# Odd filter-gradient rows first, turned copies in pieces, and new row buffers and weight-load order in the tail of an adaLN spectral block

## The chip, the cores and the metric

The kernel runs on one core of one Trainium2 chip. The core has five engines with their own instruction streams: TensorE (PE in the profile, with its weight loads as PEld), VectorE (DVE), ScalarE (ACT), GpSimd (POOL) and SyncE (SP). Each runs its instructions in order; semaphores hold an instruction back until what it needs is done. DMAs are issued here from SP and from POOL. The metric is the device time of one execution in microseconds (us); lower is better. The trace is of one execution.

## The reference

The reference runs an adaLN block with two branches forward, and then its vector-Jacobian product for a given output gradient:

```python
mod = (_silu(c) @ w_mod).reshape(c.shape[0], 6, 1, -1)
sa, ca, ga, sb, cb, gb = (mod[:, 0].copy(), mod[:, 1].copy(), mod[:, 2].copy(), mod[:, 3].copy(), mod[:, 4].copy(), mod[:, 5].copy())
h = _layernorm(x, axis=-1) * (1 + ca) + sa
x = x + ga * _A_ref(h, A_w_r, A_w_i)      # irfft2(rfft2(h) * (w_r + i w_i))
h = _layernorm(x, axis=-1) * (1 + cb) + sb
x = x + gb * _B_ref(h, B_w_gate, B_w_up, B_w_down)   # ((h@gate) * (h@up)) @ down
return x
...
_out, _vjp = jax.vjp(_f, A_x, A_w_r, A_w_i, B_w_gate, B_w_up, B_w_down, c, w_mod)
return (_out0, *[jnp.asarray(_g) for _g in _grads])
```

x is 1 x 2048 x 576 in bfloat16, the spectral filter w_r, w_i is 2048 x 289, the gated branch has 4608 features, c is 1 x 576 and w_mod is 576 x 3456. The outputs are: out_0 the forward result, out_1 the gradient of x, out_2 and out_3 the gradients of w_r and w_i, out_4, out_5 and out_6 those of the gate, up and down weights, out_7 the gradient of c (576 numbers) and out_8 the gradient of w_mod (576 x 3456, an outer product of silu(c) with the six modulation gradients).

## The kernel before

Rows of x are cut into 16 tiles of 128 (NT); the 4608 features into 36 blocks of 128 ("fb", NFB). Up to about 1230 us the kernel does the forward spectral branch and a main loop over the feature blocks, which makes the weight gradients; the change does not touch it. What follows is the tail of `build`, from line 976, with three stages and an end.

**Stage 1** (`t1_norm`, `t1_out`, `t1_turn`, about 1230 to 1316 us): per tile the backward of the second normalization, a gradient tile "gx" that POOL stores to DRAM (L1223), and its transform along the columns. **Stage 2** (`t2_*`, to about 1390): per pair of frequency lanes the transform along the rows, the product with the filter, and the way back. **Stage 3** (`t3_*`, to about 1471): per tile "sa" the inverse transform, the backward of the first normalization, and the store of the out_1 tile "ob" (L1449, on POOL). **The end**: what is left of the modulation gradients.

Into these stages is dealt the final down-projection, 1152 matmuls of 128x128 by 128x288 ("u3p", L1495), 24, 24 and 21 per step, in groups of 36 that each fill one PSUM bank; ACT copies a full bank out (L1500), VectorE scales and adds (L1508, L1509) into a tile "of3", and POOL stores it to out_0 (L1514). The very first two pairs of groups (tiles 0 and 1) run side by side, matmul by matmul. The weights come in six pieces (0 to 6, 7 to 13, 14 to 20, 21 to 27, 28 to 34 and 35 of the feature blocks; `wd_load`, L1284), and the activations in loads "hl" of 9 feature blocks by 256 rows (`hl_load`, L1288), which rotate over six buffers; the first ones are issued on POOL between the gx stores, in an order written out at L1309, and later ones on SP.

**The filter gradient** (`filter_grad`, L1324) is made in 16 units: a load "Xn" of the saved spectrum, four VectorE instructions (L1330 twice, L1331, L1332), and a result in one lane of the array "wn". Even unit 2i goes to lane i (0 to 7), odd unit 2i+1 to lane 16-i (9 to 15), unit 1 to lane 8. Before, stage 2 makes the even units (from `t2_more`), its last one once more in `t2_back`, and stage 3 the odd ones, at odd sa. Two columns of each lane are halved by POOL (`scale_ends`, L1417); lanes 0 to 8 are then stored as they are (L1443, on POOL), lanes 9 to 15 must be stored in reversed row order. For that they are first written to a DRAM scratch "gback_d" (L1523, on SP) and copied from DRAM to DRAM with the rows turned (`turned_rows`, L1539, on SP), 896 rows of 578 bytes for each of out_2 and out_3.

**The modulation gradients.** For out_8, `product_rows` (L1147) lets ACT scale a gradient row by silu(c), five row blocks for each of six sections, into one five-row tile "o8" per section; two stores on SP follow the fifth row. Four sections are made in stage 2, two rows a step (L1362), the last two (MCA, MSA) at the end. For out_7, w_mod is loaded back in sections ("wmE" of 4 sections wide in three buffers, five loads; "wmL" of 2 wide in four buffers, five loads) and VectorE multiplies and sums them (`section_sum`, L1161) into a scratch tile "pr"; small steps then make the row "gcr" (L1546 to L1564).

**Order.** For TensorE, ACT and VectorE the order in the tail is written out: `deal` (L1055) strings the collected instructions together and `in_order` ties each to the one before. SP's end is tied in the same way (`end_sp`). Elsewhere the scheduler orders POOL and SP. A buffer of a pool of n is written again only when the last reader of its content n tiles back is done, a store included: `of = o2p.tile([128, D], BF, name="of3", bufs=3)` at L1506 and the `o8` tile (one buffer) at L1150 are such places.

## Time and profile before

| what | value |
|---|---|
| time, three runs | 1525.87, 1529.7, 1531.91 us; median 1529.7 |
| profiled execution | 1528.03 us, span 1526.3 us |
| mean granted TensorE clock | 0.985 |
| TensorE busy in the span | 1460.6 us (96%) |
| VectorE busy | 1047.6 us (69%) |
| ScalarE busy | 559.5 us (37%) |
| POOL busy | 233.1 us (15%) |
| HBM read, written | 105.14 MB, 81.25 MB |
| DMA queues, share of 16 engines | from SP 51.7%, from POOL 21.9% |

"Busy" counts the time in which an engine executes; the granted clock is what TensorE's throttle allowed, 1 being full speed. A line of waits reads: engine, tile, line, then what released it, the microseconds in total, how many times, and the longest. A line of the timeline has its start, its length, the engine, the line of the program, the operation and tile, the number of instructions merged into it, and in brackets the idle time ahead of it with its releaser. "Landing" is the time from the issue of a DMA to the arrival of its last byte. A window line gives the busy microseconds (and instruction counts) of PE, PEld, DVE, ACT and POOL in that stretch, then the granted clock, the mean share of time in which the 16 DMA engines were busy, and GB/s.

### The profile page before, as it was taken

To read this page: it belongs to the slowest core of one execution; us is meant where nothing else is said; L and a number is where in the kernel's file an instruction comes from. 1 tells how busy PE (TensorE), PEld (TensorE's weight loads), DVE (VectorE), ACT (ScalarE), POOL (GpSimd) and SP (SyncE) were. 2 spreads that over 40 slices of the span, in tenths; PEclk is the share of its full clock that TensorE was granted. 3 is DMA by queue.
4 is the path that set the end of the run, shared out by engine and by line. 5 is a ranking of instruction groups with operands and counts; after the bars stand their busy time and mean duration, and the time that the engine had idled before them with its cause. 6 is when DMAs were issued, how large, how long until landed. Compare 5 with 4: busy or idle time off the path is not lost. (4 is left out here: it accounts for less than half of the span.)

```text
span 1526.3 us, 27836 instructions
## 1 busy us (share of the span) xinstructions
PE 1460.6 (96%) x10713; PEld 987.9 (65%) x10713; DVE 1047.6 (69%) x2537; ACT 559.5 (37%) x1196; POOL 233.1 (15%) x370
## 2 busy tenths in 40 slices
PE   7999999999999999999999999999999997999965
PEld 5665544666766666667666666676666675777653
DVE  7485755676766767767666777676676675497974
ACT  7566833222222222222222222222222265475541
POOL 1101211110111111112011011021110122202210
PEclk8999999999999999999999999999999999999997
DMA  9967975868776876866777687687685678836884
GB/s 336 303 192 215 241 222 157 175 137 167 171 152 126 172 150 138 156 147 152 146 154 158 132 162 162 119 172 149 132 178 111 133 208 312 286 121 186 228 245 100
DMA packets 486836, 271.12 MB, mean 178 GB/s; under 512 B 409677, under 2 KB 456910, under 8 KB 486318
## 3 DMA queue, kind: packets, MB, share of 16 engines
q1 hardware_dynamic: 459454, 170.15, 51.7%
q0 software_dynamic: 27248, 99.18, 21.9%
q8 instruction: 84, 1.38, 0.4%
q14 instruction: 50, 0.41, 0.1%
HBM read 105.14 MB, written 81.25 MB: 122 GB/s over the span
## 5 line engine op out<-in xcount | busy, mean ns | idle before, releaser
L914 DVE TENSOR_TENSOR acc<-acc,u8p 128x288 f32<-128x288 f32 (+1 forms) x1088 | 482.4, 452 | 276.7 <-PE u8p L909 272.8
L909 PE MATMUL u8p<-wT,ggT 128*128 128x288 bf16 x1152 | 327.9, 286 | 1.5 <-DVE acc L914 1.4
L909 PE MATMUL u8p<-wT,guT 128*128 128x288 bf16 x1152 | 327.6, 286 | 0.0
L870 PE MATMUL gup<-h2T,wgu 128*128 128x512 bf16 x1152 | 297.8, 379 | 0.0
L789 ACT CAST so<-u57p 128x288 bf16<-128x288 f32 x208 | 83.0, 399 | 507.2 <-PE u57p L787 507.2
L1495 PE MATMUL u3p<-wd,hl 128*128 128x288 bf16 x1080 | 152.8, 291 | 32.4 <-ACT ob L1500 22.6
L787 PE MATMUL u57p<-h2p,gg_sf 128*128 128x288 bf16 x1088 | 176.6, 286 | 0.0
L787 PE MATMUL u57p<-h2p,gu_sf 128*128 128x288 bf16 x1088 | 176.6, 286 | 0.0
L870 PEld LDWEIGHTS <-wgu 128*128 128x128 bf16 x1152 | 109.6, 98 | 97.9 <-issue 17.1
L909 PEld LDWEIGHTS <-ggT 128*128 128x128 bf16 x1152 | 112.6, 98 | 66.4 <-issue 14.0
L578 PE MATMUL u4p<-goT,wdT 128*128 128x512 bf16 x668 | 154.6, 379 | 0.8 <-ACT ghh_st L172 0.8
L1495 PEld LDWEIGHTS <-hl 128*128 128x128 bf16 x1152 | 112.6, 99 | 64.9 <-issue 32.2
L909 PEld LDWEIGHTS <-guT 128*128 128x128 bf16 x1152 | 112.7, 98 | 57.1 <-issue 2.0
L872 ACT CAST gT<-gup 128x512 bf16<-128x512 f32 x144 | 84.4, 586 | 131.4 <-PE gup L870 129.5
L787 PEld LDWEIGHTS <-hh_sf 128*128 128x128 bf16 x1152 | 112.7, 98 | 28.4
L787 PEld LDWEIGHTS <-gu_sf 128*128 128x128 bf16 x1088 | 106.5, 98 | 27.0
L787 PEld LDWEIGHTS <-gg_sf 128*128 128x128 bf16 x1088 | 106.5, 98 | 26.8
L872 ACT CAST uT<-gup 128x512 bf16<-128x512 f32 x144 | 84.4, 586 | 77.8 <-PE gup L870 77.0
L578 PEld LDWEIGHTS <-wdT 128*128 128x128 bf16 x668 | 63.6, 98 | 72.2 <-issue 6.5
L787 PE MATMUL u57p<-gonC,hh_sf 128*128 128x288 bf16 x576 | 99.7, 286 | 0.0
L885 POOL DMA_DIRECT2D hhT_d<-hhT x36 | 33.2, 923 | 373.4 <-DVE hhT L874 372.8
L172 ACT CAST ghh_st<-u4p 128x512 bf16<-128x512 f32 x102 | 58.4, 586 | 59.6 <-PE u4p L578 57.5
(270 smaller groups left out, 1694.2 us busy)
## 6 DMA issues: line engine op xcount, KB each, us to landing
hhT_d<-hhT POOLq DMA_DIRECT2D x36, 512.0 KB, 6.5
ghhT_d<-ghh_st POOLq DMA_DIRECT2D x35, 512.0 KB, 3.6
ghh<-ghhT_d POOLq DMA_DIRECT2D x35, 512.0 KB, 7.5
hl<-hhT_d SPq DMA_DIRECT2D x28, 576.0 KB, 5.6
out_dram<-woT SPq DMA_DIRECT2D x68, 128.0 KB, 2.0
wd<-in_B_w_down_dram POOLq DMA_DIRECT2D x37, 144.0 KB, 4.6
wdn<-in_B_w_down_dram SPq DMA_DIRECT2D x18, 288.0 KB, 4.7
out_dram<-so SPq DMA_DIRECT2D x36, 144.0 KB, 2.5
```

What stands on the lines that cost most here:

```text
L172: nc.scalar.copy(dst, src)
L578: nc.tensor.matmul(pt[:], lhsT=wdTs[k][:, j, m, :], rhs=goT[:, 4 * sb4:4 * sb4 + 4, m, :], start=(m == 0 and n == 5), stop=(m == n - 1))
L787: mm = nc.tensor.matmul(pw[0][:, 0:288], lhsT=sf[:, t, :], rhs=rhs_n(t, h * 288, 288), start=(t == 0), stop=(t == NT - 1))
L789: followed(mm, nc.scalar.copy(so[:, h * 288:(h + 1) * 288], pw[0][:, 0:288]))
L870: nc.tensor.matmul(pts[k][:], lhsT=wgu[:, 4 * wi_ + m, jw * 128:(jw + 1) * 128], rhs=h2T[:, ts_, m, :], start=False, stop=(m == 3))
L872: nc.scalar.copy((gT, uT)[wi_][:, th_, :], pts[k][:])
L885: nc.gpsimd.dma_start(hhT_d[:, :, fb, :].rearrange("tp f x -> f tp x"), hhT[:].rearrange("f (tp ti) p -> f tp (ti p)", ti=2))
L909: nc.tensor.matmul(pu[:, 0:288], lhsT=l_, rhs=r_, start=(k == 0), stop=(k == len(mms) - 1))
L914: summed[t] = nc.vector.tensor_tensor(out=ghb(t)[:, hs_] if fbs[-1] == NFB - 1 else dst, in0=dst, in1=pu[:, 0:288], op=ADD).ins
L1495: mm = nc.tensor.matmul(p2[ti][:, 0:288], lhsT=hls[fb // 9][:, fb % 9, ti * 128:(ti + 1) * 128], rhs=w[:, fb - f0, h * 288:(h + 1) * 288], ...
```

## The change

Five edits, all in the tail:

- **Filter gradients.** Stage 2 makes the odd units 3 to 15 (lanes 9 to 15) and unit 0, once each; stage 3 makes the even units 2 to 14 and, at its last tile, unit 1 (lanes 1 to 8). The scaling of lanes 9 to 15 and their write to gback_d are issued on POOL at tile 0 of stage 3; the turned copies follow on POOL in eight pieces of 32 row positions by 7 lanes, at tiles 3, 5, 6, 7, 8, 9, 11 and 12. Lanes 0 to 8 are scaled and stored three at a time, at tiles 4, 10 and 15.
- **Row buffers.** A product row has a tile of its own (six buffers; five others for the last section) and its own store, issued on SP.
- **Weight loads.** Weight pieces and hl loads are issued after other gx stores, three pieces and three hl loads by tile 2, and the hl buffers rotate in another order.
- **First groups.** In the two pairs of groups that run side by side, the second group's matmuls lag by six and a half feature blocks.
- **Room.** The zero tile is 32 columns wide and read by broadcast, the section sum overwrites its input, and "of3" has two buffers.

In SP's written order, the stores of section MCA's rows stand ahead of the fourth wmE load, those of MSA behind the fifth.

```diff
--- before.py
+++ after.py
@@ -986,7 +986,7 @@
         ps_cs = pool("ps_cs", 1, space=PSUM)
         ps_u3 = pool("ps_u3", 2, space=PSUM)
         tl0 = pool("tl0", 1)
-        zero = tl0.tile([128, 512], BF, name="zero")
+        zero = tl0.tile([128, 32], BF, name="zero")
         tl = pool("tl", 1)
         o2p = pool("o2p", 2)
         hlt, wds = [], []
@@ -1102,7 +1102,7 @@
         def add_zero(*banks):
 
             for cs in banks:
-                nc.tensor.matmul(cs[:], lhsT=ident[:], rhs=zero[:], start=True, stop=False)
+                nc.tensor.matmul(cs[:], lhsT=ident[:], rhs=zero[:].unsqueeze(1).to_broadcast([128, 16, 32]), start=True, stop=False)
 
         def diag(cs, cs6, off, a, b, step, w, last_, shut=True):
 
@@ -1142,17 +1142,12 @@
                 mask = ident[:, 0:DC] if m < 5 else ident[:, 128 - DC:128]
                 nc.vector.tensor_scalar(out=x[:, m * DC:m * DC + DC], in0=mask, scalar1=d[:, m:m + 1], scalar2=None, op0=MUL)
 
-        o8s = {}
-
-        def product_rows(j, m, d):
-
-            if m == 0:
-                o8s[j] = tl.tile([128, 5, D], BF, name="o8")
-            r, o8 = RM[m], o8s[j]
-            nc.scalar.activation(out=o8[r, m, :], in_=d[r, :], func=ACT.Copy, scale=sc_col[r, m:m + 1])
-            if m == 4:
-                nc.sync.dma_start(out_8[0:512, j * D:(j + 1) * D].rearrange("(m q) n -> q m n", q=128), o8[:, 0:4, :])
-                nc.sync.dma_start(out_8[512:576, j * D:(j + 1) * D], o8[64:128, 4, :])
+        def product_rows(j, m, d, pool=None):
+
+            r, r0 = RM[m], 128 * m if m < 4 else 512
+            o8 = tl.tile([128, D], BF, name="o8", bufs=6) if pool is None else pool.tile([128, D], BF, name="o8e", bufs=5)
+            nc.scalar.activation(out=o8[r, :], in_=d[r, :], func=ACT.Copy, scale=sc_col[r, m:m + 1])
+            return nc.sync.dma_start(out_8[r0:r0 + r.stop - r.start, j * D:(j + 1) * D], o8[r, :]).ins
 
         def section_load(m, j0, n, wm):
             r0 = 128 * m if m < 4 else 512
@@ -1160,7 +1155,7 @@
 
         def section_sum(m, wm, d, n, k):
             r = RM[m]
-            return nc.vector.scalar_tensor_tensor(out=pr[r, 0:n * D], in0=wm[r, :], scalar=1.0, in1=d[r].rearrange("p j n -> p (j n)"), op0=MUL, op1=MUL, accum_out=gsc[r, m, k:k + 1])
+            return nc.vector.scalar_tensor_tensor(out=wm[r, :], in0=wm[r, :], scalar=1.0, in1=d[r].rearrange("p j n -> p (j n)"), op0=MUL, op1=MUL, accum_out=gsc[r, m, k:k + 1])
 
         with ExitStack() as r1:
             c1 = pool("c1", 2, "right", stack=r1)
@@ -1290,7 +1285,7 @@
                 hl = hlp.tile([128, 9, 256], BF, name="hl2")
             else:
                 slot[0] += 1
-                hl = hlt[(0, 3, 2, 4, 1)[slot[0]] if slot[0] < 5 else (0, 3, 2, 5, 4, 1)[(slot[0] + 1) % 6]].tile([128, 9, 256], BF, name="hl")
+                hl = hlt[(0, 2, 1, 3, 4)[slot[0]] if slot[0] < 5 else (0, 2, 1, 5, 3, 4)[(slot[0] + 1) % 6]].tile([128, 9, 256], BF, name="hl")
             queued(eng, behind_, hl[:], hhT_d[nq // 4, :, 9 * (nq % 4):9 * (nq % 4) + 9, :])
             if nq == 13:
                 in_order([last[eng], ld3["gxc", "ins", 0]])
@@ -1306,7 +1301,7 @@
             return hl
 
         first_hl = []
-        for t, *loads in ((1, (0, 7)), (2, 0), (3, (7, 7)), (4, 1), (5, (14, 7)), (6, 2), (7, (21, 7), 3), (8, (28, 7), (35, 1))):
+        for t, *loads in ((1, (0, 7), 0, (7, 7), (14, 7)), (2, 1, 2), (4, (21, 7)), (5, (28, 7), (35, 1)), (7, 3)):
             for x in loads:
                 if isinstance(x, int):
                     first_hl.append(queued_load(t, hl_load, x, nc.gpsimd))
@@ -1352,7 +1347,7 @@
 
             def t2_more(k):
                 if 1 < k < NPR + 2:
-                    filter_grad(2 * pairs[k - 2])
+                    filter_grad(2 * pairs[k - 2] + (pairs[k - 2] > 0))
                 if k in (1, 2):
                     spread((dcb, dga)[k - 1])
                 if k == 2:
@@ -1386,8 +1381,6 @@
 
             def t2_back(n):
                 plane_back(T["GB"], sds[n % 2], pairs[n], nrest, utB, new)
-                if n == NPR - 1:
-                    filter_grad(2 * pairs[n])
 
             pipeline(NPR, [t2_cols, t2_rows, t2_filter, t2_back], 2)
         T["IF"] = load_table(tl0, "IF", "tA", nc.gpsimd)
@@ -1434,13 +1427,22 @@
             own["gn", sa] = [gn_in]
             if sa % 2:
                 mark = traced()
-                filter_grad(sa, nc.sync)
+                filter_grad(sa + 1 if sa < NT - 1 else 1, nc.sync)
                 own["unit", sa] = of_engine(mark, "DVE")
-            if sa == 3:
-                scale_ends(0, NPR + 1)
-            if sa > 3 and sa % 2 == 0:
-                c, a = sa // 2 % 2, 3 * (sa // 4 - 1)
-                nc.gpsimd.dma_start((o2_v, o3_v)[c][:, a:a + 3, :], wn[:, c, a:a + 3, 0:DF])
+            if sa == 0:
+                scale_ends(NPR + 1, NT)
+                for c in range(2):
+                    nc.gpsimd.dma_start(gback_d[c], wn[:, c, NPR + 1:NT, 0:DF])
+            if sa in (4, 10, 15):
+                a = {4: 0, 10: 3, 15: 6}[sa]
+                scale_ends(a, a + 3)
+                for c, o_v in enumerate((o2_v, o3_v)):
+                    nc.gpsimd.dma_start(o_v[:, a:a + 3, :], wn[:, c, a:a + 3, 0:DF])
+            if sa in turned_at:
+                c, q = turned_at.index(sa) // 4, turned_at.index(sa) % 4 * 32
+                nc.gpsimd.dma_start(turned_rows((o2_v, o3_v)[c])[:, q:q + 32, :], gback_d[c].rearrange("k j f -> j k f")[:, q:q + 32, :])
+
+        turned_at = (3, 5, 6, 7, 8, 9, 11, 12)
 
         def t3_sums(sa):
             ob = c3.tile([128, D], BF, name="ob1")
@@ -1461,7 +1463,6 @@
         rB.close()
         secp = pool("secp", 1, "right", stack=rA)
         wme = [secp.tile([128, 4 * D], BF, name="wmE%d" % k) for k in range(3)]
-        pr = secp.tile([128, 4 * D], BF, name="pr")
         secq = pool("secq", 1, "right", stack=rA)
         hlp = pool("hlp", 4, "right", stack=rA)
         with behind([ld3["last"]]):
@@ -1488,13 +1489,12 @@
                     p2[ti] = ps_cs.tile([128, 512], FP32, name="u3q", tag="cs" + "AB"[n3 // 2 % 2]) if tp_ == NT // 2 - 1 and n3 % 2 else ps_u3.tile([128, 512], FP32, name="u3p")
                     if h == 0:
                         obs[ti] = o2p.tile([128, D], BF, name="ob3", bufs=4)
-                for fb in range(NFB):
+                mms = {}
+                for fb, (ti, h) in sorted(((fb, g_) for fb in range(NFB) for g_ in group), key=lambda x: 2 * x[0] + 13 * x[1][0]):
                     f0, w = wd_part(fb)
-                    mms = []
-                    for ti, h in group:
-                        mm = nc.tensor.matmul(p2[ti][:, 0:288], lhsT=hls[fb // 9][:, fb % 9, ti * 128:(ti + 1) * 128], rhs=w[:, fb - f0, h * 288:(h + 1) * 288], start=(fb == 0), stop=(fb == NFB - 1))
-                        mms.append(mm)
-                for (ti, h), mm in zip(group, mms):
+                    mms[ti] = nc.tensor.matmul(p2[ti][:, 0:288], lhsT=hls[fb // 9][:, fb % 9, ti * 128:(ti + 1) * 128], rhs=w[:, fb - f0, h * 288:(h + 1) * 288], start=(fb == 0), stop=(fb == NFB - 1))
+                for ti, h in group:
+                    mm = mms[ti]
                     if (tp_, ti, h) == (NT // 2 - 1, 1, 1):
                         continue
                     followed(mm, nc.scalar.copy(obs[ti][:, h * 288:(h + 1) * 288], p2[ti][:, 0:288]))
@@ -1503,7 +1503,7 @@
                     if h == 0:
                         continue
                     t = 2 * tp_ + ti
-                    of = o2p.tile([128, D], BF, name="of3", bufs=3)
+                    of = o2p.tile([128, D], BF, name="of3", bufs=2)
                     if t < NT - 1:
                         nc.vector.tensor_tensor(out=of[:], in0=obs[ti][:], in1=gb_h[:], op=MUL)
                         nc.vector.tensor_tensor(out=of[:], in0=of[:], in1=x1t[:, ti, :], op=ADD)
@@ -1512,31 +1512,28 @@
                             nc.vector.tensor_tensor(out=of[:, hs_], in0=src, in1=gb_h[:, hs_], op=MUL)
                             nc.vector.tensor_tensor(out=of[:, hs_], in0=of[:, hs_], in1=x1t[:, ti, hs_], op=ADD)
                     nc.gpsimd.dma_start(o0_v[:, t, :], of[:])
-                then_dve[mms[-1].ins.name] = of_engine(mark, "DVE")
+                then_dve[mms[group[-1][0]].ins.name] = of_engine(mark, "DVE")
         end_sp += [i_ for i_ in nc.cur_bb.bb.instructions[last_mark:] if i_.engine == mybir.EngineType.SP]
         end_pe = []
         with tc.issue_after(ld3["last"]):
-            scale_ends(NPR + 1, NT)
             mark_sp = traced()
             wmL = [section_load(m, MSA, 2, secq.tile([128, 2 * D], BF, name="wmL", bufs=4)) for m in range(4)]
-            for c in range(2):
-                nc.sync.dma_start(gback_d[c], wn[:, c, NPR + 1:NT, 0:DF])
             end_sp += of_engine(mark_sp, "SP")
+            rows_sp = {}
             for at, (j, d) in zip((12, 12), ((MCA, dca), (MSA, dsar))):
                 mark_pe = traced()
                 spread(d)
-                for m in range(5):
-                    product_rows(j, m, d)
+                rows_sp[j] = [product_rows(j, m, d, secq if j == MSA else None) for m in range(5)]
                 end_pe.append((at, pe_since(mark_pe), of_engine(mark_pe, "Activation")))
+            end_sp += rows_sp[MCA]
             mark = traced()
             for m in range(5):
                 section_sum(m, wmE[m][0], early, 4, 0)
                 if m < 2:
                     wmE.append(section_load(m + 3, MGA, 4, wme[m]))
                     end_sp.append(wmE[-1][1])
+            end_sp += rows_sp[MSA]
             mark_sp = traced()
-            for c, o_v in enumerate((o2_v, o3_v)):
-                nc.sync.dma_start(turned_rows(o_v), gback_d[c].rearrange("k j f -> j k f"))
             for m in range(5):
                 section_sum(m, wmL[m][0], ends, 2, 1)
                 if m == 0:
```

## The prediction

> **What bounds the kernel now.** I read, in this order: the page for the whole, the windows for the stages, the waits of the tail in two halves, and the timelines of the engines at the longest waits. The profiled execution took 1528.03 us, 1526.3 of them span; it lies 1.7 below the median of the three runs shown (1529.7), and the sum below is made against 1528.0. The page's busy lines:
>
> ```profile
> PE 1460.6 (96%) x10713; PEld 987.9 (65%) x10713; DVE 1047.6 (69%) x2537; ACT 559.5 (37%) x1196; POOL 233.1 (15%) x370
> ```
>
> TensorE bounds the main loop to about 1230 us, which the change does not enter. The change can only take idle time out of the tail or put some in. Windows of the tail (busy time of PE, PEld, DVE, ACT, POOL, then granted clock, DMA share, GB/s):
>
> ```profile
> 1260.00:1270.00 10.00, 6.89 (x65) 4.99 (x63) 6.87 (x21) 6.66 (x14) 3.86 (x8) 1.00 1.04 376
> 1270.00:1280.00 10.00, 5.37 (x37) 3.94 (x37) 3.69 (x12) 3.14 (x6) 2.48 (x4) 0.79 1.05 382
> ...
> 1380.00:1390.00 10.00, 9.77 (x71) 7.44 (x71) 9.69 (x25) 7.32 (x19) 0.54 (x1) 0.83 0.30 91
> ...
> 1440.00:1450.00 10.00, 9.98 (x93) 7.86 (x91) 9.86 (x28) 6.73 (x19) 1.90 (x4) 1.00 0.71 198
> ...
> 1480.00:1490.00 10.00, 0.00 (x0) 0.00 (x0) 0.00 (x0) 0.00 (x0) 0.00 (x0) 0.53 1.19 168
> 1490.00:1500.00 10.00, 1.76 (x8) 1.11 (x8) 3.40 (x4) 4.24 (x7) 0.00 (x0) 0.50 0.96 218
> ```
>
> TensorE is short of data at 1260 to 1280, VectorE sets the pace from 1430 (9.86 of 10), and at 1480 to 1490 nothing computes while the DMA engines are full. Who ends the waits, first in 1250 to 1370, then in 1370 to 1527:
>
> ```profile
> PE u3p L1495 <- DMA wd<-in_B_w_down_dram: 6.3, 2, 3.9
> ACT o L1152 <- issue: 2.1, 1, 2.1
> PE fq L212 <- ACT es L223: 2.0, 1, 2.0
> PE u3p L1495 <- ACT ob L1500: 2.1, 2, 1.1
> ```
>
> ```profile
> PE u3p L1495 <- ACT ob L1500: 20.5, 1, 20.5
> ACT o L1152 <- DMA out_dram<-o: 18.3, 1, 18.3
> DVE pr L1163 <- DMA wmE<-in_w_mod_dram: 16.8, 1, 16.8
> ACT o L1152 <- issue: 3.6, 1, 3.6
> PE fq L212 <- ACT b_GY L219: 3.1, 1, 3.1
> DVE ob L1053 <- DMA out_dram<-ob: 2.9, 2, 1.5
> ```
>
> The three long rows are one event: ACT's second set of product rows needs the buffer of the first, its store (issued at 1480.29) lands at 1494, and ACT's bank copies and TensorE's last groups stand behind it. The same event on PE, and POOL's queue in stage 3:
>
> ```profile
> 1498.24 5.90 PE L1495 MATMUL u3p<-wd,hl 128*128 128x288 bf16 x36 [20.46 <-ACT ob L1500]
> 1503.98 4.57 PE L1495 MATMUL u3q<-wd,hl 128*128 128x288 bf16 x36
> ```
>
> ```profile
> 1410.17 1.57 POOL L1443 DMA_DIRECT2D out_dram<-wn  x2
> 1411.74 0.57 POOL L1449 DMA_DIRECT2D out_dram<-ob  x1
> 1412.30 2.27 POOL L1443 DMA_DIRECT2D out_dram<-wn  x3
> 1414.57 0.57 POOL L1449 DMA_DIRECT2D out_dram<-ob  x1
> ```
>
> **The change, part by part.**
>
> *Stage 1: loads earlier, first groups interleaved.* The weight pieces for features 7 to 20 go out behind tile 1's store, not tiles 3 and 5: by their other waits about 1242, where the trace has 1249.8 and 1256.6. The fourth piece goes at about 1253 (1263.7 before; it landed 8.5 later and ended the 3.87 wait), the fifth at 1261 (1269.9; the 2.45 wait). By that 8.5 they land at 1262 and 1270, some 7 us ahead of their uses, though bank 0's lead wants them 6 or 7 matmuls (0.8 us) sooner. Gone: 3.87 and 2.45, and the slow matmuls behind them: 14 took 3.38 us at 1278.9, where 24 take 3.10 at full clock (0.13 each), 1.6 lost; the other three groups up to 1283, counted the same way, 1.6 more. Bank 0 now ends 7 matmuls (0.9 us) ahead of bank 1, longer than its two copies (0.70), so the two 1.07 waits on ACT's copies go. 3.9 + 2.4 + 3.2 + 2.1 = 11.6; I take 0.8 off for a leftover wait: **-10.8**. Ends: -3 (the DMA share is already 1.0 at 1250 to 1280, and a load moved forward delays others) and -12.
>
> *Stage 2: one buffer per product row (six), a store each.* ACT's waits of 2.1 and 3.6 on the one five-row tile's store go, and with them PE's 2.0 (1342.6) and 3.1 (1380.2) behind ACT. Of the second only 2.7 counts, since VectorE (9.83 of 10 us busy there) paces the last pairs: **-4.7**, ends -2 and -5. Thirty stores instead of twelve are issued on SP; the two of a row set took 6.0 and 21.5 us of SP waiting, behind which only prefetches stand. The odd gradient unit replaces the even one with the same 2.3 us of VectorE and the same load. The duplicate unit at the stage's end saves 2.3 us where VectorE was idle (3.11 of 10 busy at 1390 to 1400): 0. The 32-column zero, read 16 times over: 0, the same matmul count; no row shows the broadcast read. Nor has one the section sum written in place: 2.56 us each as before.
>
> *Stage 3: the turned rows' path moves here from the end.* After tile 0 POOL issues eight scalings and two 506 KB copies to gback_d, then eight turned pieces of a quarter copy. The two copies collide with hl loads issued at 1392.8 and needed at 1398 (landing 5.6): +2.5, ends 0 and 5.
> The new wait is on of3, two buffers for three. VectorE's third product of the stage, right after tile 3's unit (ends 1415.7), needs the first one's store to have landed. POOL issues that store only after four scalings that wait for the same unit (1.6 us), three pieces, two wn stores and an ob store (0.5 to 0.8 each, 4.2 together): issued 1421.5. Landing: 3.0 (the of stores of the quiet end) to 9.1 (the ob store behind the six wn stores). So VectorE stands for 8.8 to 14.9; I take 12.2, by the 6.4 median of the ob stores in 1405 to 1428, same bytes and queue. It replaces the 2.9 of ob waits, and nothing absorbs it: VectorE is 97% busy afterwards, TensorE follows it, bank copies and stores queue behind. 12.2 - 2.9 + 2.5 + about 0.7 clock = **+12.5**, ends +5 and +18. Two dozen later POOL issues of 0.5 to 0.8 hide in POOL's idle 6 us of 10.
>
> *End.* No gback or turned copies on SP (second turned copy: about 8 us alone after 1498.4), five buffers for the last rows: ACT does not wait 18.3 and TensorE does not wait 20.5. The fourth w_mod piece is issued at about 1477.5 instead of 1483.4, as soon as the first sum frees its buffer, without 1 MB of gback and the first turned copy beside it; by 10.2 landing (median of wmE loads in the tail) it is there at 1488, so the fourth sum goes at 1488, and the fifth at 1491.5 by its own load, not 1510.0 behind the two 4.57 groups. From that sum to the end of the span stays 16.3. 1510.0 - 1491.5 = **-18.5**. Ends: -10 (wmE lands at 12.8 and a wait of 5 on loads remains) and -21.
>
> Sum: -10.8 - 4.7 + 12.5 - 18.5 = -21.5: 1506.5 against 1528.0, and 1.7 for the median: **1508**.
>
> **A rule weighed.** Rows first: a wn store of 384 rows took a median 7.7 from issue to landing in 1405 to 1428; a quarter of a turned copy is 224 rows. The Trainium skill, DMA: Bandwidth & Descriptors, Anatomy of one DMA, gives a transfer on GpSimd's path about 2.0 us and its bytes over 436 GB/s: 2.3 for a 129 KB piece, and an estimate by that page of 2.3 for the of store also. By it VectorE's wait would be 8.1, stage 3 would end 4 us earlier, and the sum would be 1504. The trace has no landing under 3.0 for that size, so my sum stays with the rows. The same page speaks against the change in its advice to merge small transfers (Rules for kernel authors): pieces and rows that each pay their own completion. That is the first rival, by rows.
>
> **The rivals.**
> 1. *The stores ahead land one after another* (ends slower). If POOL's queue moved one small-row transfer at a time, the first of store would sit behind five of them, 5 x 7.7 = 38 us, then its own 6.4: VectorE stands about 50, not 12.2. Sum -21.5 + 38 = +16.5: about 1546. It decides from a stand of 34 us. For it: the ob store behind six wn stores took 9.1, three times 3.0. Against: those six, issued in 5.9 us, would then have held it 40. Chance 0.06.
> 2. *Loads early do not help stage 1* (DMA full from 1250: 0.99 to 1.05). What comes early displaces x1c, yc and gx traffic; -3 instead of -10.8: 1516. Against: 1240 to 1250 is at 0.70, and two of the pieces move there. Chance 0.16.
> 3. *The end keeps a wait on w_mod*: four weight loads of 576 KB, four wmL and the rows share the engines at 1470 to 1490; -10: 1516. Chance 0.16.
> 4. *VectorE's of wait is short*, landing 3.0 and no loss at gback: stage 3 at +6, 1502. Chance 0.17.
> 5. *Stage 1 and end both fall short*, or the wait is 20: 1523 to 1535, no measurable change or a little slower. Chance 0.06.
>
> **The numbers.** My forecast has 0.39. The 8-in-10 range runs 1496 (case 4 with the end at -21 and stage 2 at -5) to 1524 (cases 2 and 3 together, 1524). Half a per cent, 7.6 us, is what a measurement of this kernel can tell from no change: below 1522 counts as faster. Cases 2, 3, 4 and mine make 0.88; of them 0.02 fall inside the bound; case 5 adds 0.05 to that and 0.01 slower; case 1 with 0.06 is slower: 0.86, 0.07, 0.07.
>
> **What would show it.** Right: no wait of TensorE on wd before 1285; no ACT wait on a store of o; one VectorE wait of 9 to 15 on a store of "of" in stage 3, a few us after tile 3's unit; TensorE's last wait on a bank copy under 4; stage 3 still at VectorE 9.8 of 10; the turned pieces landing in about 4 to 8 each. Wrong: a VectorE wait over 30 there, or repeated ones on "of" (two buffers too few for every pair), waits of TensorE on hl at 1395 to 1405 above 5, or a fourth w_mod piece that lands after 1495.

## The result, and the profile after

The changed kernel takes 1523.67 us (median of 11 runs, 1519.43 to 1527.22) against 1530.83 for the kernel before (11 runs, 1524.78 to 1532.76): a ratio of 0.9957, 95% interval 0.9942 to 0.9973. A second set of runs on another occasion gave 0.9955 (0.9939 to 0.9971). By the ratio that is 6.6 us faster, on the forecast side, but a third of the 21.5 forecast, and inside the half per cent that the prediction called hard to measure: it counted a time below 1522 as faster. The profiled execution has a span of 1521.9 us, 4.4 under that of before.

To see where the time went I cut the tail of each trace at the same five points: the last matmul of the main loop (u8p), the first matmul of stage 2 (T_RF), the first of stage 3 (T_IF), the first spread of the end (spp from ends), and the end of the span. These points come from the timeline of TensorE; "end" here starts at the spread.

| us | stage 1 | stage 2 | stage 3 | end |
|---|---|---|---|---|
| before | 85.6 | 71.7 | 79.4 | 55.7 |
| after, first profile | 79.7 | 67.6 | 96.7 | 42.8 |
| after, second profile | 77.9 | 70.1 | 96.4 | 41.8 |
| forecast of the difference | -10.8 | -4.7 | +12.5 | -18.5 |
| difference, first and second profile | -5.9, -7.7 | -4.2, -1.7 | +17.3, +17.0 | -12.9, -13.9 |

The main loop adds +1.3 and 0.0, from its own scatter. All four terms have the forecast sign, and all four are worse than forecast. These stage times scatter. Of the kernels of the next section, e1, e2, e3, e8, e9 and e11 (short for their full names) leave stage 1 as in the changed kernel, and it took 78.4 to 84.0 us in their profiles; e2, e4 and e5 leave stage 3, and it took 91.9 to 96.5. So a difference of a few us between two profiles is checked against the timed runs.

The page, first the busy line after (PE, PEld, DVE, ACT, POOL):

```profile
PE 1462.7 (96%) x10713; PEld 988.4 (65%) x10713; DVE 1044.9 (69%) x2533; ACT 560.9 (37%) x1196; POOL 242.4 (16%) x387
```

TensorE does the same 10713 matmuls; only its idle time has moved. The windows of the changed kernel (busy PE, PEld, DVE, ACT, POOL, granted clock, DMA share, GB/s):

```profile
1390.00:1400.00 10.00, 5.42 (x26) 3.33 (x25) 3.70 (x9) 1.97 (x4) 0.00 (x0) 0.70 0.89 313
1420.00:1430.00 10.00, 0.00 (x0) 0.00 (x0) 3.08 (x9) 1.79 (x6) 1.93 (x4) 0.56 0.66 171
1480.00:1490.00 10.00, 7.93 (x54) 5.70 (x53) 7.74 (x8) 5.66 (x10) 1.11 (x2) 0.86 1.02 294
```

The empty stretch of before, at 1480 to 1490, is filled; a new one stands at 1420 to 1430, and half ones at 1260 (TensorE busy for 4.88 of 10 us) and 1390. Their waits, from the list for 1230 to 1370 and then from that for 1370 to the end:

```profile
POOL hl L1274 <- DMA x1c<-x_d: 7.5, 1, 7.5
DVE gxr L1045 <- DMA gx_d<-gxr: 5.7, 2, 4.0
PE u3p L1495 <- ACT wo_l L822: 5.1, 1, 5.1
```

```profile
DVE of L1508 <- DMA out_dram<-of: 12.5, 1, 12.5
PE yp L282 <- ACT zz L277: 12.2, 1, 12.2
PE u3p L1495 <- ACT ob L1500: 4.8, 1, 4.8
PE u3p L1495 <- DMA hl<-hhT_d: 4.6, 1, 4.6
ACT o8e L1149 <- DMA out_dram<-of: 4.3, 1, 4.3
DVE wmE L1158 <- DMA wmE<-in_w_mod_dram: 3.9, 1, 3.9
```

The waits on wd (6.3), on ACT's copies in stage 1 (2.1), on es and b_GY in stage 2 (2.0 and 3.1) and the three long ones of the end (20.5, 18.3, 16.8) are gone or down to 0.2 (the copies) and 3.9 (VectorE's on w_mod), as forecast. Four others stand in their place: 5.1 in stage 1, 4.6 and 12.5 in stage 3, 4.8 at the end.

### The profile page after: what moved, and what is told of

The parts are those of the page before. It is cut to its first block, busy times and chain, and to the rows that moved or that the text cites. A ratio compares the mean times of both kernels' runs of the same rounds, so it can differ in the third digit from the quotient of the medians.

```text
span 1521.9 us, 27874 instructions
## 1 busy us (share of the span) xinstructions
PE 1462.7 (96%) x10713; PEld 988.4 (65%) x10713; DVE 1044.9 (69%) x2533; ACT 560.9 (37%) x1196; POOL 242.4 (16%) x387
## 4 chain that ended last, share of the span: by engine, by line
PE 83%; DMA 5%; DVE 5%; issue 4%; POOL 1%; ACT 1%; SPq 1%; POOLq 0%; DVEq 0%; ACTq 0%
PE u57p L787 27%; PE u8p L909 19%; PE gup L870 17%; PE u4p L578 9%; PE u3p L1495 3%; PE gup L865 3%; DMA hl<-hhT_d 2%; DMA h2p<-in_A_x_dram 1%; PE fq L651 1%; DVE gwt L1325 1%; PE fq L212 1%; DMA x1t<-x_d 1%; PE fq L276 1%; PE fq L256 1%; DMA out_dram<-so 1%
```

## The experiments

Each is named with the ratio of its time to that of the kernel before, taken beside it. The kernel before had medians from 1525.7 to 1528.9 in the three sets of runs, so times of different sets are compared by their ratios. Stage times are cut as above; where an edit is long, the lines that matter are shown.

**The store of "of".** POOL's queue around VectorE's wait, changed kernel:

```profile
1414.11 0.97 POOL L1413 TENSOR_SCALAR wn<-wn 128x3 bf16<-128x3 bf16 x4 [2.23 <-DVE wn L1326]
1415.03 0.76 POOL L1443 DMA_DIRECT2D out_dram<-gback_d  x1
1415.79 1.53 POOL L1440 DMA_DIRECT2D out_dram<-wn  x2
1417.32 2.08 POOL L1443 DMA_DIRECT2D out_dram<-gback_d  x3
1419.39 1.15 POOL L1514 DMA_DIRECT2D out_dram<-of  x2
```

VectorE finished tile 3's unit at 1414.4 and stood until 1426.9. The store that it waits for was ready at 1382 (its L1509 ran at 1381.6) and went out at 1419.4, behind everything that POOL had been given first. The experiment e1_of moves only that: an order for POOL in which the stores of tiles 6 and 7 follow the third turned piece.

```diff
+        in_order(turned[2:3] + [of_st[6], of_st[7], st[0], turned[3], st[1], st[2]] + ends_of[4][:4]
+                 + turned[4:5] + ends_of[4][4:] + turned[5:8] + [of_st[8], st[3], st[4], st[5], st[6], of_st[9], st[7]])
```

(`of_st`, `st`, `turned`, `ends_of[4]` are the stores of "of" and "ob", the turned pieces, and the scalings with the wn stores at tile 4.)

> The changed kernel with one difference: on POOL the stores of output tiles 6 and 7 go out right after the third turned piece, not behind the scalings, the pieces four to eight and the two wn stores. Theory (the 12.5 us in which VectorE waits for a store of "of" at 1414 to 1427 is only that store's place in POOL's queue): that wait is gone, ob tile 5 may wait up to 3 for its buffer instead, and the end comes 8 to 12 us earlier than in the changed kernel (about 1512 to 1516 by its median of 1523.7). Rival (POOL and the DMA engines are what is short around 1415 to 1425, so the wait only changes its name): VectorE waits 8 or more on ob stores instead, and the time moves by under 4.

Measured 0.9914 (0.9895 to 0.9934), 1512.0 us; stage 3 86.0 instead of 96.7. Of VectorE's waits in this kernel, 1375 to 1520, the longest on a store is:

```profile
DVE ob L1053 <- DMA out_dram<-ob: 5.0, 1, 5.0
```

No wait on a store of "of" is left. What is late next is the ob buffer (5.0, expected up to 3), so 7.5 of the 12.5 us are left as a gain. The timed runs agree: against the ratio of the changed kernel, 0.9955 to 0.9957, the gain is 6 to 7 us, a little under the 8 to 12 expected. The 10.7 us by which stage 3 is shorter than in the changed kernel's profile are partly its scatter, as the wait on hl also fell there from 4.6 to 2.7 with gback where it was. The theory's cause held, its size was somewhat too large; the rival's wait of 8 or more did not come.

**Three buffers instead of two** (e11_of_three) tells the queue's place from the buffer count.

```diff
-                    of = o2p.tile([128, D], BF, name="of3", bufs=2)
+                    of = o2p.tile([128, D], BF, name="of3", bufs=3)
```

> The changed kernel with three "of" buffers instead of two, as before the change. Theory (the store's place in POOL's queue, not the buffer count, is the cause): the first store is still issued behind the pieces, so VectorE's wait at tile 3 goes, but its next product, at tile 6 or 7, waits for the store of the tile before in the same queue: one wait of 5 to 9, stage 3 at 87 to 92 instead of 96.5. Rival (the third buffer is all that is missing): no wait on "of" over 1, stage 3 at 83 to 86, as with e1_of or better.

Measured 0.9954 (0.9938 to 0.9971), stage 3 89.7. VectorE's timeline there:

```profile
1440.61 0.46 DVE L1508 TENSOR_TENSOR of<-ob,gb_h 128x576 bf16<-128x576 bf16 x1 [6.45 <-DMA out_dram<-of]
```

One wait of 6.5, several tiles later: a third buffer postpones the wait for a store that goes out late. The whole time did not follow: in the profiled execution stage 1 took 84.0 (below), and TensorE waited 7.5 us on hl in stage 3; whether the timed ones had that too isn't known.

**gback later** (e3_gback_late). In the changed kernel the two gback copies go out on POOL at 1376.7 and 1378.7, and TensorE waits for hl from 1391 on. TensorE and SP, changed kernel:

```profile
1395.29 1.62 PE L1495 MATMUL u3p<-wd,hl 128*128 128x288 bf16 x6 [4.58 <-DMA hl<-hhT_d]
1396.70 1.66 PE L276 MATMUL zp<-T_IF,ut_t 128*128 128x289 bf16 x6
1398.16 1.89 PE L1495 MATMUL u3p<-wd,hl 128*128 128x288 bf16 x7
```

```profile
1383.98 7.34 SPq L1274 DMA_DIRECT2D hl<-hhT_d  x4
```

The load that TensorE waits for is the first of these four. It was issued at 1384.0 and landed 11.3 us later, as the wait ended. In the kernel before, where gback is not in the way, the first two hl loads of this place landed in 4.1 and 5.6.

```diff
+        in_order([of_st[6], of_st[7], st[0]] + ends_of[0] + [st[1], st[2]] + ends_of[4] + [of_st[8], turned[0], st[3],
+                 turned[1], st[4], turned[2], st[5], turned[3], st[6], of_st[9], turned[4], st[7], turned[5], st[8],
+                 turned[6], st[9], turned[7]])
```

(`ends_of[0]` is the scaling of lanes 9 to 15 and the two writes of gback.)

> The changed kernel with gback written behind the store of ob tile 0 (about 1396 instead of 1377), the turned pieces one by one between the later ob stores, and the out_0 stores each ahead of them, so that the wait on "of" is taken away as in e1_of too. Theory (the 4.6 us wait of TensorE on hl at 1391, and about 3 of slow matmuls behind it, come from the 1 MB of gback in 578-byte rows that delays the gxc and hl loads): no hl wait over 1 us at 1385 to 1400 and the end 5 to 8 us earlier than e1_of. Rival (the hl loads are late for SP's own order, since each issue waits for the landing of the one eight before): the hl wait stays at 3 or more and the end is within 2 of e1_of.

Measured 0.9864 (0.9850 to 0.9879), 1505.05 us; stage 3 79.7, 17.0 less than in the changed kernel and 6.4 less than in e1_of. By the ratios the gain over e1_of is 7.6 us, as the theory had it (5 to 8). TensorE's wait on hl from 1380 to 1470 in this kernel:

```profile
PE u3p L1498 <- DMA hl<-hhT_d: 0.3, 1, 0.3
```

The hl wait fell from 4.6 to 0.3, the first two hl loads landed in 4.8 and 5.4, and stage 3 is back at the 79.4 of before. So the order on POOL accounts for stage 3's loss: the same DMAs, placed between others, cost next to nothing there. The rival, SP's own order, is out for this wait, since the load was issued 1.6 us after the start of stage 3, as in the kernel before. How much of the gain over e1_of is gback's and how much comes from the turned pieces, which this edit spreads as well, was not separated. Two later kernels with this order, e9_best_late and e7_all_fixed, have hl waits of up to 3.2 and 2.1 near 1420 to 1427, and stage 3 at 80.7 and 82.7.

**The end: late rows** (e2_rows_late).

```diff
-            for at, (j, d) in zip((12, 12), ((MCA, dca), (MSA, dsar))):
+            for at, (j, d) in zip((12, 60), ((MCA, dca), (MSA, dsar))):
```

> The changed kernel with one difference: the spread and the five product rows of section MSA stand behind 60 matmuls of the last groups instead of 12. Theory (at the end TensorE's 4.8 us and the 1.7 us of slow clock behind it come from ACT, which holds bank copies behind the first MSA row, and that row waits 4.3 for its buffer, freed by the last ob store): TensorE's wait at 1488 to 1493 falls under 1 us, the last group starts 5 to 6 us earlier, the end comes 3.5 to 6 earlier. Rival (the fourth w_mod piece, issued at 1492, sets the end): its sum still ends at 1500.5 as before, the tile behind it follows, and the end moves by at most 3.4; by a stricter form of it, not at all.

Measured 0.9934 (0.9912 to 0.9957), 1514.95 us; the end 38.8 instead of 42.8. TensorE's longest wait from 1460 on:

```profile
PE gcp L1555 <- DVE gcd L1549: 5.7, 1, 5.7
```

The 4.8 us wait is gone and the end 4.0 shorter than in the first profile of the changed kernel, 3.0 shorter than in the second (41.8). The theory's wait is shown; the sizes, 3.5 to 6 by the theory and at most 3.4 by the rival, do not tell the two apart, and the ratios, 0.9934 and 0.9955, have overlapping intervals. What limits next is what the rival named: VectorE waits 8.2 for the fourth w_mod piece (3.9 in the changed kernel), and the last matmul 5.7 for VectorE's sums.

**The w_mod loads first** (e9_best_late). SP's own timeline of the changed kernel has the reason to try it:

```profile
1475.61 2.19 SPq L1274 DMA_DIRECT2D hl<-hhT_d  x4
1477.84 2.71 SPq L1154 DMA_DIRECT2D wmL<-in_w_mod_dram  x4
1481.06 10.90 SPq L1150 DMA_DIRECT2D out_dram<-o  x5
1492.06 1.14 SPq L1154 DMA_DIRECT2D wmE<-in_w_mod_dram  x2
```

Five small stores took SP 10.9 us. Each waits for a DMA that has nothing to do with it: SP's list of waits puts 8.3 us on hl loads, over four stores, and 0.2 on a wmL load. The order fits a wait for the DMA eight before on the same queue: counted back eight places, the first four stores meet the four hl loads and the fifth the first wmL load. No run varies that number.

```diff
-            end_sp += rows_sp[MCA]
             mark = traced()
...
-            end_sp += rows_sp[MSA]
+            end_sp += rows_sp[MCA] + rows_sp[MSA]
```

together with the edits of e2_rows_late and e3_gback_late.

> The changed kernel with the edits of e2_rows_late and e3_gback_late, and with the fourth and fifth w_mod loads ahead of all ten row stores in SP's order. Theory (in the end those two loads stand behind five row stores that each wait for the landing of the DMA eight before, 10.9 us of SP; with the bank copies free, the sums are what is left): the fourth load goes out at the end of its first sum, 5 or more earlier, VectorE does not wait for it, and the end falls from 38.8 (e2_rows_late) to 34 to 37; the whole 3 to 8 us under e3_gback_late's ratio of 0.986, so 0.981 to 0.984. Rival (TensorE's last four groups, 18.3 us, and their copies are the bound): the end stays at 38 to 39 and the ratio at 0.983 to 0.985.

Measured 0.9818 (0.9803 to 0.9833), 1501.71 us, the lowest ratio of this study; the end 39.2. VectorE in this kernel:

```profile
1481.42 2.56 DVE L1158 SCALAR_TENSOR_TENSOR wmE<-wmE,early 128x2304 bf16<-128x2304 bf16 x1 [9.41 <-DMA wmE<-in_w_mod_dram]
```

The fourth load did go out right after the first sum, at 1466.2, but landed 15.2 us later, behind 3.5 MB of hl and wmL loads. The ratio is in the theory's range, but the end did not shorten beyond the 38.8 of the late rows alone; there the rival's number, 38 to 39, nearly held, though not its reason: VectorE waits 9.4 for the load, not for the last groups. Against e3_gback_late (end 42.1) the end is 2.9 shorter.

**Stage 1.** Three runs were spent on the 5.1 us. The chain in the changed kernel, by the waits above and the timelines: the last out_6 store, issued on SP at 1245.06, landed in 9.6 us (2.7 before); the second hl load takes its buffer, so POOL stood 7.5 at it until 1255.3 (the list names a load of x1c that landed about then; in the changed kernel's two profiles and in e1, e4, e5 and e11 the second hl load went out 0.6 to 0.7 us after the out_6 store had landed); the gx stores of tiles 3 and 4, behind it in the queue, went out together at 1256.3 (at 1249.2 and 1252.7 before); VectorE waited 4.0 for their ring buffer, ACT 3.8 for VectorE, and ACT's last wo_l copy ran at 1267.5 instead of 1261.6. It frees the bank that the second of the two interleaved groups needs. First, one MB less ahead of the second hl load (e4_wd2_behind_hl):

```diff
-        for t, *loads in ((1, (0, 7), 0, (7, 7), (14, 7)), (2, 1, 2), (4, (21, 7)), (5, (28, 7), (35, 1)), (7, 3)):
+        for t, *loads in ((1, (0, 7), 0, (7, 7)), (2, 1, 2, (14, 7)), (4, (21, 7)), (5, (28, 7), (35, 1)), (7, 3)):
```

> The changed kernel with one difference: the weight piece for features 14 to 20 is issued behind the second and third hl loads, not ahead of tile 2's store. Theory (3 MB of early loads keep the last out_6 store, whose buffer the second hl load takes, from landing until 1255, so that load is issued at 1255.3 and TensorE waits 5.1 for it at 1263 to 1268): the second hl load is issued 3 to 5 us earlier, the 5.1 wait falls to 1 to 2, and the end comes 3 to 5 us earlier. Rival (the DMA engines are full from 1250 whatever the order): the wait of 5 moves to the piece that now comes later, wd for features 14 to 20, and the time moves by under 1.5.

Measured 0.9969 (0.9956 to 0.9982), no faster than the changed kernel; stage 1 80.7. The second hl load went out 3.0 us earlier (1252.2), as expected, but TensorE still waited 5.8 for wo_l, which was not expected, and VectorE 6.2 for a gx store. The load itself was not what TensorE waited for. That made the chain above the next theory, and e5_gx_first tests it:

```diff
-        for t, *loads in ((1, (0, 7), 0, (7, 7), (14, 7)), (2, 1, 2), (4, (21, 7)), (5, (28, 7), (35, 1)), (7, 3)):
+        for t, *loads in ((1, (0, 7), 0, (7, 7), (14, 7)), (4, 1, 2, (21, 7)), (5, (28, 7), (35, 1)), (7, 3)):
```

> The changed kernel as it is, on the same chip as the three beside it, as their reference. Every theory expects the ratio of 0.9957 and the waits of its first profile: 5.1 of TensorE at 1263 to 1268, 4.6 on hl at 1391, 12.5 of VectorE on "of", 4.8 of TensorE at 1488, each within some 2 us.

> The changed kernel with one difference: the second and third hl loads stand behind the gx stores of tiles 3 and 4 on POOL, not ahead of them. Theory (POOL stands 7.5 us at the second hl load, whose buffer the last out_6 store has to leave; two gx stores wait behind it, VectorE waits 4.0 for their ring buffer, ACT 3.8 for VectorE, and TensorE 5.1 for the bank that ACT's last wo_l copy frees): VectorE's wait on gx stores at 1244 to 1272 falls under 1, ACT's last wo_l copy ends near 1262, TensorE's wait there falls to 1 or less, and stage 1 (last main-loop matmul to first stage-2 matmul, 79.7 now) is 4 to 6 shorter. Rival (full DMA engines: what is not waited for here is waited for at the next load): a wait on hl or wd of 3 or more appears between 1262 and 1285 and stage 1 is under 2 shorter.

The changed kernel came out as expected (0.9955; waits 4.0 in stage 1, 5.1 on hl, 5.4 at the end, 12.8 for TensorE behind "of"). e5_gx_first: 0.9956 (0.9940 to 0.9972), stage 1 77.7 beside 77.9. TensorE's waits in stage 1 there:

```profile
PE u3p L1495 <- DMA hl<-hhT_d: 4.6, 3, 3.5
PE u3p L1495 <- ACT wo_l L822: 0.5, 1, 0.5
```

The theory's chain is real, and the rival's outcome came: the wait on wo_l fell to 0.5, and over the runs it follows VectorE's longest wait on a gx store (at most 2.3 and 0.5 here, 4.0 and 5.1 in the changed kernel, 6.2 and 5.8 in e4_wd2_behind_hl, 9.0 and 9.4 in e11_of_three). But taking it away brought a wait of 3.5 on hl instead, and no time. That the loads as a whole decide stage 1 is the likely reading, since the DMA share is 1.04 at 1250 to 1260 in the changed kernel and the same bytes must come; it is not shown, as no run takes bytes out. How much of stage 1's gain is the order of loads and how much the interleaving wasn't separated.

**All four repairs** (e7_all_fixed: e2_rows_late, e3_gback_late, e5_gx_first together).

> The changed kernel with the edits of e2_rows_late, e3_gback_late and e5_gx_first together. Theory (they are four separate waits: 5.1 in stage 1, 4.6 on hl, 12.5 on "of", 4.8 at the end, each with slow matmuls behind it): the gains add up, 17 to 24 us under the changed kernel, a ratio of 0.975 to 0.982 to the kernel before. Rival (a common limit, VectorE's work in stage 3 or the DMA engines, takes over): under 13 us.

Measured 0.9851 (0.9817 to 0.9886): the ratio misses the theory's 0.975 to 0.982, and the median, 1504.85 against 1522.30 beside it, lies at the lower end of its 17 to 24 us. Stage 3 is 82.7, with two hl waits of 1.5 and 2.1 that e3_gback_late did not have, and the end 39.7. By the ratios the three edits give 14, 3 and 0 us alone and 16 together, so within the noise they add, and the one of stage 1 is none. What was expected from stage 1 is missing from the sum.

**The parts alone.** e6_rows_alone is the kernel before with only the row buffers and what makes room for them, the small zero tile and the section sum in place. The line of the buffers:

```diff
-            o8s[j] = tl.tile([128, 5, D], BF, name="o8")
+            o8 = tl.tile([128, D], BF, name="o8", bufs=6) if pool is None else pool.tile([128, D], BF, name="o8e", bufs=5)
```

> The kernel before with the row buffers alone (a tile and a store for each product row, the small zero, the section sum in place); loads, filter gradients and turned copies as before. Theory (the two waits of ACT in stage 2 and the 18.3 at the end come from the one five-row buffer): stage 2 (first stage-2 matmul to first stage-3 matmul, 71.7 before) is 3.5 to 5 shorter, the 20.5 wait of TensorE falls under 8, and since the fourth w_mod piece is still issued behind ten row stores and gback the end is 5 to 10 shorter than the 55.7 of before. Rival (the end is bound by the jam of gback, turned copies and w_mod loads whatever the buffers): the end shortens by under 3.

Measured 0.9890 (0.9872 to 0.9908), 1513.1 us: more than twice the gain of the whole change. Stage 2 70.0 (1.7 shorter, not 3.5 to 5: the waits on es and b_GY are gone, but a wait of 2.7 on hl, up to 1327.2, stands there), the end 44.5 (11.2 shorter, expected 5 to 10). TensorE's waits from 1330 on:

```profile
PE gcp L1552 <- DVE gcd L1546: 9.5, 1, 9.5
...
PE u3p L1489 <- ACT ob L1494: 3.4, 1, 3.4
```

The 20.5 has become 3.4 with gback and the turned copies still at the end. Stage 1, not edited here, took 82.8 beside the 85.6 of before, by scatter. e8_units_back is the other side, the changed kernel without its first edit (even units in stage 2, odd ones in stage 3, gback and the turned copies on SP at the end, as before):

```diff
-                    filter_grad(2 * pairs[k - 2] + (pairs[k - 2] > 0))
+                    filter_grad(2 * pairs[k - 2])
...
+            for c in range(2):
+                nc.sync.dma_start(gback_d[c], wn[:, c, NPR + 1:NT, 0:DF])
...
+            for c, o_v in enumerate((o2_v, o3_v)):
+                nc.sync.dma_start(turned_rows(o_v), gback_d[c].rearrange("k j f -> j k f"))
```

> The changed kernel without its first edit: even units in stage 2, odd ones in stage 3, lanes 0 to 8 stored at tiles 4 to 14, gback and the two turned copies on SP at the end, as before; row buffers, load order, interleaved groups and two "of" buffers stay. Theory (moving the turned path into stage 3 costs there more than it saves at the end: stage 3 took 96.5 us with it and 79.4 to 80.0 without, the end 42.3 with it and 44.5 without): stage 3 is 80 to 84, the end 43 to 47, and the whole is 10 to 15 us faster than the changed kernel, a ratio of 0.986 to 0.990. Rival (the two "of" buffers alone bring the wait, wherever the turned pieces are): VectorE waits 8 or more on "of" in stage 3 and the whole gains under 6.

Measured 0.9869 (0.9853 to 0.9886), 1509.1 us; stage 3 81.3, the end 43.0. VectorE's longest waits in stage 3:

```profile
DVE ghr L285 <- ACT ye L284: 5.1, 2, 4.5
DVE ob L1053 <- DMA out_dram<-ob: 4.9, 2, 2.7
```

None on "of", with the same two buffers (one of 3.4 stands earlier, up to 1315.6 in stage 2, as one of 2.6 to 2.9 does in the changed kernel; with three buffers there is none). So in stage 3 the buffer count costs nothing without the pieces, and the first edit as written costs 0.9955 / 0.9869 = 1.0087, about 13 us. What e8_units_back has over e6_rows_alone is above all the order of loads and the interleaved groups (besides them two "of" buffers, the order of the row stores on SP, and one unit that is no longer made twice): 0.9890 against 0.9869, about 3 us, with intervals that overlap. That is all that these runs give to the part of the change that was to bring 10.8. Last, e10_units_back_late is e8_units_back with the late rows and early w_mod loads:

> e8_units_back with the late MSA rows and the early w_mod loads of e9_best_late. Theory (with buffers, loads and order right, it matters little where the turned path runs, as 1 MB of gback at the end then collides with the w_mod loads for some us): the end is 36 to 42 and the whole within 6 us of e9_best_late, slower of the two. Rival (the end is clean only without gback there): the end stays at 43 to 46.

Measured 0.9855 (0.9837 to 0.9872), the end 45.0: its rival held on the end (43 to 46), while the whole, 5.9 us slower than e9_best_late, is just within the theory's 6. VectorE waits 11.9 for the fourth w_mod piece and 4.3 for wmL, with gback ahead of them. Against e9_best_late (39.2) the cleared end is worth 5.8 us, which is what the first edit can give, once stage 3 does not pay for it.

## Why the prediction was right and wrong

- **Direction and mechanisms: right; size: wrong.** The waits that were to go went; the 1523.67 lies at the upper edge of the range (1524), and the gain is 6.6 of 21.5. It is the outcome of the fifth rival, stage 1 and the end both falling short, which had 0.06, and of a stage 3 worse than forecast. The failure lies in the sizes of three terms: stage 1 (-5.9 for -10.8), stage 3 (+17.3 for +12.5) and the end (-12.9 for -18.5).
- **"VectorE stands for 8.8 to 14.9; I take 12.2": right.** It stood 12.5; the store was issued at 1419.4, 5.0 after the unit's end (5.8 worked out), and landed about 7 later (6.4 taken). The two small errors cancelled. e1_of shows that moving the store gains 6 to 7 us by the timed runs, since 5.0 of the 12.5 came back at the ob buffer. The ways that the first and fourth rivals drew, a stand of 50 or of under 9, did not occur.
- **"The two copies collide with hl loads ...: +2.5, ends 0 and 5": the step that failed in stage 3.** The wait on hl was 4.6 and 5.1 in the two profiles (2.7 to 5.7 over the other kernels with gback in that place and the same two "of" buffers), and the slow matmuls behind it weigh as well: 6 took 1.62 us, then 6 of T_IF 1.66 and 7 more 1.89, where the same groups take 0.90, 0.92 and about 0.9 to 1.0 later in the stage, some 2.3 in all. Together near 7, outside the range set for this term; with the 12.5 of VectorE's wait and the 2.9 of ob waits that it replaced, that makes 16.6 of the 17.3 measured. The step took hl's landing as the 5.6 of before and added a wait of 2.5; with gback beside it the load landed in 11.3. SP's third hl load of that place also stood 5.0 us behind gxc loads, but it is not the one that TensorE waited for.
- **"I take 0.8 off for a leftover wait": the step that failed in stage 1.** The old waits went (11.6 by the sum), but one of 4.0 to 5.1 came, and its own slow matmuls: 15 took 3.55 us. The step set the second and third weight pieces at "about 1242", which came true (1242.1), and the fourth at about 1253; it went out at 1257.4, behind the late hl load. It did not ask what a late landing of SP's out_6 store does to POOL, and through gx stores to VectorE, ACT and the bank. The second rival, that the DMA engines are full whatever the order, was closer to the truth than its 0.16: e4_wd2_behind_hl and e5_gx_first both moved loads and gained nothing, and e8_units_back, which has this part of the change, is only about 3 us under e6_rows_alone, which lacks it.
- **The end: "The fourth w_mod piece is issued at about 1477.5 ... as soon as the first sum frees its buffer": wrong, but not what cost the time.** It went out at 1492.1, because I had counted SP's row stores as free issues, and each waited for an earlier load to land. But the sum that waits for it could begin 5.8 us after the issue, where 10.2 was taken, by luck: 18.8 us after the spread, forecast 17.4. In e9_best_late the load did go out early, and landed late. What cost the time is the wait of ACT on the last ob store for the first MSA row (4.3; the list names a store of "of", but that one landed only at 1490.1, and the last ob store at 1488.3, just before ACT went on), then TensorE's 4.8 and 1.7 of slow matmuls. Through them VectorE waited 3.4 for a bank copy ahead of the fifth sum, which began 25.7 after the spread, forecast 20.9. The prediction put "TensorE's last wait on a bank copy under 4" but gave it no price. e2_rows_late takes that wait away: -4.0, or -3.0 against the second profile; there the late fourth piece is what VectorE waits for.
- **Its own signs.** Of the signs of being wrong, two came: the fourth w_mod piece landed after 1495 (at 1497.9), and the wait on hl was above 5 in the second profile (5.1). TensorE's last wait on a bank copy was 4.8 and 5.4, not under 4. The rest of the signs of being right came, but the turned pieces landed in a median of 8.2, slightly above the 4 to 8.
- **Stage 2: right in its waits, its size near the low end.** -4.2 in the first profile; -1.7 in the second, just short of the end of -2, with an hl wait of 2.9, up to 1320.7. ACT's waits on the old row store are in neither.
- **What the sum did not ask.** It credited the end with "no gback or turned copies on SP" and five buffers as one term of 18.5. e6_rows_alone shows that the buffers give 11.2 of the 12.9 alone, and e8_units_back has an end of 43.0 without the first edit, so that this edit bought 0 to 2 us at the end and paid 15 to 17 in stage 3.
- **Slips in the working.** The 3.0 for the landing of a store of "of" is a median over ten of them from 1380 on; the last two of the kernel before, issued at 1510.3 and 1522.4, landed in 2.0, so "no landing under 3.0" is misread and the wait's lower end would be 7.8. The lower end of the range, 1496, does not follow from the case named for it, which gives 1499. A wait of 20 alone would give 1516, not the 1523 of the fifth rival.

The rule weighed in the prediction had a shorter landing for the store of "of". The measured landing of the store that decides was about 7 us, so the sum's rows were nearer there than the estimate of 2.3 us worked out from the Trainium skill, DMA: Bandwidth & Descriptors, Anatomy of one DMA; that estimate does come near the two landings of 2.0 at the quiet end of the kernel before. Its advice to merge small transfers (Rules for kernel authors) would speak against one store for each row, and yet the row buffers alone brought 1.1%; the 10.9 us that SP spent on five of these stores were waits for earlier loads to land.

## What to carry to other kernels

Moving transfers off a crowded place saves only what they cost there, and it puts them ahead of something else in an in-order queue: before pricing the gain, write out the destination queue in its compiled order and look for the store or load behind them that another engine waits for. Do the parts of a bundle one at a time; here one part gave 15.7 us alone and another cost 13. And when a wait is removed by reordering loads while the DMA engines are full, look for it at the next load, where it came back here (5.1 on a bank, then 3.5 on hl).

## What the runs showed of the hardware

- A queue's later issue can wait for a landing of no concern to it. Five stores of 72 to 144 KB took SP 10.9 us in the changed kernel, and the landing that ended each wait is that of the DMA eight places before it on SP's queue.
- Landing times stretch with what is ahead more than with size: w_mod pieces of 576 KB took a median of 7.1 us in the end of the changed kernel, and one of them 15.2 in e9_best_late, behind 3.5 MB issued in the 7 us before; an hl load of the same size landed in 11.3 with gback's 1 MB ahead of it, and in 4.8 without.
- TensorE's matmuls ran slow also behind waits shorter than I had thought: 6 took 1.46 us behind a wait of 2.97 in e2_rows_late, and in e1_of, behind one of 2.69, the first 6 ran at full speed (0.91) and the next 6 did not (1.49). The Trainium skill, TensorE: Matmul & The Clock Gate, Part 1, puts the idle time after which the clock halves at about 3.4 us. By these records gaps under that were enough, down to 2.15 us: after a wait of that length ahead of the spread in the changed kernel, 12 matmuls took 3.09 us, where 12 take 1.6 at full speed, and the granted clock from 1479 to 1483 is 0.57.
